# Retention and a mixture of experts on one core: the expert stage issued in program order, with its rows gathered one expert ahead

## The chip, the core and the metric

The kernel runs on one core of a Trainium2 chip. Five engines work there side by side, each through its own queue in order: TensorE (PE, matmuls and transposes into PSUM), VectorE (DVE), ScalarE (ACT), GpSimd (POOL) and SyncE (SP). SP issues most DMAs, POOL the indirect ones (gathers and scatters of rows by index). The metric is the device time of one execution in microseconds; the median of several executions counts. In the profile, L216 is line 216 of the kernel, and PEld is PE's loading of weights, which runs beside its matmuls.

## The reference

Two steps. Retention: for every batch and head a state decays by gamma and collects k times v, and the output is q times the state. Its result, as 3072 rows of 512, goes to eight experts. Each row goes to the one expert whose embedding lies nearest; that expert's two layers are applied to it and the result is scaled by the softmax weight of that expert.

```python
for t in range(S):                       # B, H, S, D = 4, 8, 768, 64
    state = gamma[None, :, None, None] * state + np.einsum('bhd,bhe->bhde', k[:, :, t], v[:, :, t])
    y[:, :, t] = scale * np.einsum('bhd,bhde->bhe', q[:, :, t], state)
...
N, D = x.shape                           # 3072, 512; E, F = 8, 1024
logits = xn @ en.T / tau
expert_idx = np.argmax(logits, axis=1)
...
gate_w = probs[np.arange(N), expert_idx]
for e in range(E):
    mask = expert_idx == e
    h = np.maximum(x[mask] @ w1[e], 0.0)
    out[mask] = gate_w[mask, None] * (h @ w2[e])
```

## The kernel before

**Retention** takes the first 150 us: 24 chunks of 128 tokens, four batches of six chunks. Every chunk's result is written to a table of rows in DRAM (`xd`), its logits are computed, and counts and ranks place each token in the list of its expert. The first expert starts early, on 288 of its 416 rows (`EARLY`); its other 128 (`LATE`) are known only when the last chunk is placed. The generator `products` yields the first layer's products for the early rows one at a time, and `run(m)` takes m of them to fill PE while the last chunk is chosen, ranked and counted (`counting`, which also sorts the experts by their number of tokens and makes the index lists `tidx` for gathering and `sidx` for scattering). The late rows then go through the first layer as rows (`hr`, two halves of 512 columns), are transposed, and join the early ones in `hh` and `hl`.

**The experts** follow in order of their number of tokens, with fixed capacities of 416, 416, 408, 400, 392 and three times 384 rows (`CAPS`). All products are made in three parts for precision: each weight piece of 128 x 1024 is split into a high part (`whi`, a copy on ACT, L191) and a rest (`wlo`, a subtraction on DVE, L192), and so are the rows (`xh`, `xl`) and the hidden values (`hh`, ACT's ReLU at L219; `hl`, DVE at L220). An expert has eight pieces, four for each layer. `load_piece` asks for the next piece on SP (`raw`, six buffers in two pools), `split_piece` splits it (nine pairs of buffers).

- First layer (`first_layer`, L216): eight blocks of 128 hidden units, 12 products each, through four PSUM banks (`psc0`, `psc1`, `py`, `pst`) that `bank` gives in turn.
- Second layer, the first five experts (`layer2`, L1024): four quarters of 128 output columns, 24 products each. DVE transposes each quarter into `yt` (L1026). `finish` copies `yt` into rows (`og`, 16 DMAs on SP, L1034), POOL multiplies by the gates (L1040) and scatters to the output (L1046). Where a capacity is no multiple of 32, the bank's last columns are zeroed first (L1018).
- Second layer, the last three (`layer2_rows`, L1059): three groups of 128 rows; DVE applies the gate (L1061) and POOL scatters.
- The next expert's rows: `gather` (POOL, L959) brings rows from `xd` into `xr`; `to_quarters` writes them to DRAM (`xs`, L969 and L971) and reads them back as `xg` (L980) in a form that DVE's transpose of 32 x 32 blocks turns into columns (`xt`, L1005); `xh` and `xl` follow (L1010, L1011). `xr` has one buffer.

Gates: `gates` sums the squares of the rows, takes their norm, scales the logits (`zd`), and turns them into `gate`, one weight per token. It is written transposed (`gT`) to `gd` and as a column into `xd`. The first two experts gather their gates from `gd` (`gather_gates`, L991), the others find theirs in the gathered rows.

**What sets the order.** Up to the late rows, all engines issue in the order of the program text (`manual_schedule` over all five engines). In the expert stage only SP and POOL do; PE, DVE and ACT are ordered by a scheduler that simulates the program and lets instructions pass each other:

```python
        cx.enter_context(tc.manual_schedule(engines={mybir.EngineType.SP, mybir.EngineType.Pool}))
```

Work written under the two schedules can still be merged by the scheduler. In the text, expert e's turn begins with the gather for expert e + 1, then come the blocks of its first layer with a step of the former expert's `finish` after each and a split and a load after every second, and `to_quarters` for e + 1 after the fifth and the seventh block; then the quarters of its second layer, with a split and a load each.

## Time and profile before

| what | us |
|---|---|
| median of 3 executions | 470.42 |
| lowest, highest | 466.7, 471.93 |
| the profiled execution | 465.52 |
| its span, from the first to the last instruction | 463.7 |
| PE busy in it | 425.4 |
| expert stage: first product of expert 1 to the last product | 191.2 to 450.8 |

A row of the timeline has its start, its duration, engine, line and operation, what it writes from what, and in brackets how long the engine was idle ahead of it and what ended that. An `x8` behind a row means eight instructions merged. A row of the chain of waits has start, duration and what it was. A matmul's duration overlaps the next one's; the distance of starts tells its cost. The clock is TensorE's as granted (1.00 is full speed).

### The profile page before, as it was taken

The numbers are of one execution on the slowest core, as the hardware profiler recorded it, in microseconds if no ns is written. First come the engines' busy times: TensorE is split into PE (matmuls) and PEld (weight loads), VectorE is DVE, ScalarE is ACT, GpSimd is POOL, SyncE is SP. The second block draws the span as 40 slices with busy tenths as digits, with TensorE's granted clock in tenths as the row PEclk, the third lists the DMA queues.
The fourth block names the chain that finished last, engine by engine and source line by source line (L and its number), as shares of the span: only waits on it lengthen the run. The fifth ranks groups of instructions, "written<-read, shape, count | busy, mean of one in ns | idle before, by whom it ended". The sixth has DMA issues, their size and how long they took to land.

```text
span 463.7 us, 8893 instructions
## 1 busy us (share of the span) xinstructions
PE 425.4 (92%) x3230; PEld 381.2 (82%) x3230; DVE 266.7 (58%) x583; ACT 197.9 (43%) x467; POOL 201.4 (43%) x196
## 2 busy tenths in 40 slices
PE   8999999999989889899998999999799999979980
PEld 4787788787868869799997999999799889849860
DVE  5644687868779765764573484293383575346110
ACT  3567668665655152624243253262252353133100
POOL 2545667565545032067282362552553643402010
PEclk9999999999999899999999899999899999999995
DMA  8999999999742236959947948957877892591010
GB/s 200 232 235 241 253 218 260 252 232 248 173 114 47 71 116 208 317 127 289 297 121 214 303 156 203 293 222 187 256 270 188 247 343 77 164 253 66 1 48 20
DMA packets 124441, 89.99 MB, mean 194 GB/s; under 512 B 61680, under 2 KB 106120, under 8 KB 124388
## 3 DMA queue, kind: packets, MB, share of 16 engines
q1 hardware_dynamic: 119972, 75.59, 61.5%
q0 software_dynamic: 4416, 13.75, 9.5%
q8 instruction: 27, 0.44, 0.4%
q14 instruction: 26, 0.21, 0.1%
HBM read 65.89 MB, written 19.39 MB: 184 GB/s over the span
## 4 chain that ended last, share of the span: by engine, by line
PE 32%; DMA 29%; DVE 16%; issue 6%; SPq 6%; ACT 4%; POOL 3%; POOLq 0%; DVEq 0%; ACTq 0%
DMA raw<-in_moe_w_dram 7%; PE psc L216 6%; DMA xg<-xs 5%; DMA xs<-xr 3%; DMA out_dram<-og,sidx 3%; DMA xr<-xd,tidx 3%; PE py L216 3%; PE py L355 3%; DVE wlo L192 2%; SPq L1034 2%; PE pst L216 2%; DMA hh<-in_q_dram 2%; PE psc L1024 2%; PE py L346 2%; PE py L1024 2%
## 5 line engine op out<-in xcount | busy, mean ns | idle before, releaser
L192 DVE TENSOR_TENSOR wlo<-raw,whi 128x1024 fp32r<-128x1024 f32 x59 | 71.8, 1245 | 52.8 <-ACT whi L191 52.4
L191 ACT CAST whi<-raw 128x1024 fp32r<-128x1024 f32 (+1 forms) x69 | 65.0, 984 | 55.5 <-DMA raw<-in_moe_w_dram 55.2
L1046 POOL DMA_INDIRECT out_dram<-og,sidx x29 | 36.1, 1245 | 97.1 <-DMA out_dram<-og,sidx 39.0
L1040 POOL TENSOR_SCALAR og<-og,gt 128x512 f32<-128x512 f32 (+4 forms) x20 | 37.8, 1889 | 37.3 <-DMA og<-yt 36.1
L216 PE MATMUL psc<-xh,whi 128*128 128x384 f32 (+5 forms) x128 | 44.1, 345 | 1.5 <-ACT xh L1010 1.5
L216 PE MATMUL psc<-xl,whi 128*128 128x384 f32 (+5 forms) x128 | 44.3, 346 | 0.7 <-DVE xl L1011 0.7
L216 PE MATMUL psc<-xh,wlo 128*128 128x384 f32 (+5 forms) x128 | 43.8, 342 | 0.0
L280 POOL TENSOR_TENSOR ks<-kin,cst 128x512 f32<-128x512 f32 x23 | 25.1, 1090 | 33.7 <-DMA kin<-in_k_dram 16.4
L959 POOL DMA_INDIRECT xr<-xd,tidx x25 | 29.5, 1179 | 23.3 <-DVE ssq L1073 16.1
L318 DVE TENSOR_TENSOR pm<-psc,cst 128x512 f32<-128x512 f32 x48 | 30.8, 682 | 10.4 <-PE psc L311 10.2
L1024 PE MATMUL psc<-hh,whi 128*128 128x416 f32 (+3 forms) x80 | 29.3, 373 | 6.7 <-ACT hh L219 5.8
L383 ACT ACTIVATE sq<-x 128x128 bf16<-128x128 f32 x96 | 29.8, 310 | 12.4 <-DVE x L369 10.1
L1010 ACT CAST xh<-xt 128x384 fp32r<-128x384 f32 (+4 forms) x28 | 13.8, 522 | 47.7 <-DVE xt L1005 47.7
L220 DVE SCALAR_TENSOR_TENSOR hl<-psc,hh 128x384 fp32r<-128x384 f32 (+5 forms) x32 | 17.0, 549 | 25.5 <-ACT hh L219 25.5
L219 ACT ACTIVATE hh<-psc 128x384 fp32r<-128x384 f32 (+5 forms) x32 | 15.4, 487 | 36.2 <-PE psc L216 36.2
L1024 PE MATMUL psc<-hl,whi 128*128 128x416 f32 (+3 forms) x80 | 28.7, 361 | 0.1
L1005 DVE STREAM_TRANSPOSE xt<-xg 128x416 f32<-128x416 f32 (+1 forms) x28 | 15.3, 573 | 23.4 <-DMA xg<-xs 23.4
L1024 PE MATMUL psc<-hh,wlo 128*128 128x416 f32 (+3 forms) x80 | 28.7, 361 | 0.0
L311 PE MATMUL psc<-qT,kT 64*128 64x128 f32 x384 | 28.0, 285 | 0.5 <-ACT kT L300 0.5
L355 PE MATMUL py<-pm,vin 128*64 128x128 f32 x368 | 27.3, 280 | 1.0 <-DVE pm L318 0.9
L311 PEld LDWEIGHTS psc<-qT,kT 64*128 64x128 f32 x384 | 23.4, 187 | 4.3 <-issue 3.1
L216 PEld LDWEIGHTS psc<-xh,whi 128*128 128x128 f32 x128 | 24.8, 194 | 2.4 <-ACT xh L1010 2.2
(296 smaller groups left out, 1075.9 us busy)
## 6 DMA issues: line engine op xcount, KB each, us to landing
raw<-in_moe_w_dram SPq DMA_DIRECT2D x60, 512.0 KB, 6.5
vin<-in_v_dram SPq DMA_DIRECT2D x24, 256.0 KB, 4.8
xd<-x SPq DMA_DIRECT2D x48, 128.0 KB, 3.9
kin<-in_k_dram SPq DMA_DIRECT2D x23, 256.0 KB, 4.6
hh<-in_q_dram SPq DMA_DIRECT2D x11, 512.0 KB, 5.8
xs<-xr SPq DMA_DIRECT2D x7, 768.0 KB
xg<-xs SPq DMA_DIRECT2D x16, 208.0 KB, 3.9
og<-yt SPq DMA_DIRECT2D x60, 48.0 KB, 5.1
```

The costliest lines, as they stand in the source:

```text
L191: nc.scalar.copy(out=hv, in_=rv)
L192: eng.tensor_tensor(out=lv, in0=rv, in1=hv.bitcast(F32), op=ALU.subtract)
L216: nc.tensor.matmul(acc[:, :w], a[:, f], x[:, kt, cols], start=(n == 0), stop=(n == 3 * KT - 1))
L280: eng.tensor_tensor(out=scaled[n][:, h], in0=loaded[n][0][:, h], in1=sc[:, h], op=ALU.mult)
L311: nc.tensor.matmul(psc[par][:, j, :], kT[r, j, :], qT[r, j, :], start=True, stop=True)
L318: nc.vector.tensor_tensor(out=pm, in0=psc[par], in1=C("causal").unsqueeze(1).broadcast_to([P, KT, P]), op=ALU.mult)
L355: nc.tensor.matmul(py[a * D:(a + 1) * D, j, :], vi[:, h, :], pt[a][:, j, :], start=(c == 0 and j == 0), stop=True, skip_group_check=True)
L383: nc.scalar.activation(out=sq, in_=xo[:, g], func=AF.Square, accum_out=ssq4[:, n, g:g + 1])
L959: nc.gpsimd.indirect_dma_start(out=xr[:n, j, :], out_offset=None, in_=xd[:, :], in_offset=bass.IndirectOffsetOnAxis(ap=tidx[:n, j, e:e + 1 ...
L1024: nc.tensor.matmul(acc[:, :c], a[:, f], x[:, kt, :c], start=(n == 0), stop=(n == 3 * FT - 1))
L1040: nc.gpsimd.tensor_scalar(out=og[:n, j], in0=og[:n, j], scalar1=gts[e][:n, j:j + 1], scalar2=None, op0=ALU.mult)
L1046: nc.gpsimd.indirect_dma_start(out=out[:, :], out_offset=bass.IndirectOffsetOnAxis(ap=sidx[:n, j, e:e + 1], axis=0), in_=og[:n, j, :], in_ ...
```

## The change

1. The expert stage is issued in program order on all five engines, and the text is written in the order wanted: within a block of the first layer the split and the load of a weight piece stand after the block's products and ahead of its ReLU; in a quarter of the second layer come products, split, the next expert's columns (in pairs, both transposes ahead of both subtractions), the quarter's own transpose, and the load. Four loads stand ahead of the first expert's second layer, not six.
2. Rows are gathered one expert ahead: while expert e works, `gather(e + 2)` is issued behind the first step of `to_quarters(e + 1)`, which moves to the first block (the second step to the third block). The steps of `finish` fall on the other blocks.
3. The zeroing of the banks' last columns (`bank2`) moves to the end of the first layer for three of the four quarters.
4. `gates` moves up, to the late rows of the first expert, and is cut into steps: squares and norm ahead of the late rows, the exponential after their first half, the sum and its transpose after the second. `gather_gates` for experts 0 and 1 moves up to the first expert; `gt` has three buffers.
5. 12 of the early products run ahead of the counts. The late rows' first layer is kept in `sbd`, the retention state's two buffers, and no longer in the retention pool's `qs`.
6. The first expert's first quarter of layer 2 is cut into columns 0 to 288 and 288 to 416.
7. One set of four banks serves everything (`bank()`), and the raw pieces change pools one piece later.

The core of the diff:

```diff
+        run(R[3])
         todo2 = counting()
-        for _ in range(19):
+        for i in range(19):
             next(todo2)
-            run(2)
+            run(2 if i < 15 else 0)
...
-        run(R[3])
+        run(DF)
+        gate_steps = gates()
+        next(gate_steps)
...
-            hr.append(ap_.tile([P, H, D], F32, name="qs").rearrange("p h d -> p (h d)"))
+            hr.append(sbd[len(hr)].rearrange("p j d -> p (j d)"))
             nc.scalar.copy(out=hr[-1][:LATE], in_=acc[:LATE])
             split_piece()
-        run(DF)
+            next(gate_steps)
...
-        raw_pool = lambda g: (rp, rp2)[(g - NPE) // 3 % 2]
+        raw_pool = lambda g: (rp2, rp)[(g - NPE - 1) // 3 % 2]
...
-        cx.enter_context(tc.manual_schedule(engines={mybir.EngineType.SP, mybir.EngineType.Pool}))
+        cx.enter_context(tc.manual_schedule(engines={
+            mybir.EngineType.PE, mybir.EngineType.DVE, mybir.EngineType.Activation, mybir.EngineType.Pool,
+            mybir.EngineType.SP}))
         steps = iter(())
+        gather(1)
+        to_go = to_quarters(1)
         for e in range(NE):
...
             if e == 0:
                 hh, hl = hh0, hl0
-                for _ in range(3):
+                for _ in range(4):
                     load_piece()
-                gate_steps = gates()
+                next(to_go)
                 next(gate_steps)
-                for _ in range(3):
-                    next(todo, None)
-                    load_piece()
+                gather_gates(0)
+                gather(2)
+                gather_gates(1)
             else:
...
+                to_go = to_quarters(e + 1) if nxt else iter(())
                 for ft in range(FT):
-                    for _ in first_layer(e, ft, bank("acc"), *xTs[e], hh, hl, slice(0, CAPS[e])):
-                        pass
-                    next(steps, None)
+                    products = first_layer(e, ft, bank(), *xTs[e], hh, hl, slice(0, CAPS[e]))
+                    for _ in range(3 * KT):
+                        next(products)
+                    if ft == FT - 1 and CAPS[e] % P:
+                        accs += [bank2(e) for _ in range(KT - 1)]
                     if ft % 2 == 1:
-                        weights()
-                    if ft in (4, 6):
-                        next(todo, None)
+                        split_piece()
+                        load_piece()
+                    next(products, None)
+                    if ft == 0:
+                        next(to_go, None)
+                        if e + 2 < NE:
+                            gather(e + 2)
+                    if ft == 2:
+                        next(to_go, None)
+                    else:
+                        next(steps, None)
...
                 for dt in range(KT):
-                    layer2(e, dt, hh, hl, yt)
-                    if nxt:
-                        for kt in ((), (0, 1), (2, 3), ())[dt]:
-                            xT_piece(e + 1, kt)
-                    with tc.issue_after(evac.ins) if e == 0 else nullcontext():
-                        weights()
+                    cols = [slice(0, EARLY), slice(EARLY, CAPS[e])] if (e, dt) == (0, 0) else [slice(0, CAPS[e])]
+                    acc = accs[dt]
+                    layer2(e, dt, hh, hl, acc, cols)
+                    split_piece()
+                    if nxt and dt in (1, 2):
+                        xT_pieces(e + 1, (2 * dt - 2, 2 * dt - 1))
+                    to_yt(e, dt, acc, yt)
+                    if (e, dt) == (0, 0):
+                        next(to_go)
+                    load_piece()
                 steps = finish(e, yt, og)
             else:
                 for j, n in groups_of(e):
-                    layer2_rows(e, j, n, hh, hl, og)
-                    if nxt:
-                        for kt in ((0,), (1, 2), (3,))[j]:
-                            xT_piece(e + 1, kt)
+                    acc = layer2_rows(e, j, n, hh, hl)
                     for _ in range((2, 1, 1)[j]):
-                        weights()
+                        split_piece()
+                    if nxt and j > 0:
+                        xT_pieces(e + 1, (2 * j - 2, 2 * j - 1))
+                    rows_out(e, j, n, acc, og)
+                    for _ in range((2, 1, 1)[j]):
+                        load_piece()
```

Three places in the instructions. First ACT, from the last blocks of expert 2's first layer (408 columns) into its second layer; `raw` pieces of 128x1024 belong to a first layer, those of 128x8x4x32 to a second. Before:

```order
L219 ACTIVATE hh_3382<-psc1_3508 128x408
L219 ACTIVATE hh_3382<-py_3529 128x408
L191 CAST whi_3642<-raw_3367 128x1024
L191 CAST whi_3683<-raw_3426 128x1024
L191 CAST whi_3726<-raw_3486 128x1024
L219 ACTIVATE hh_3382<-pst_3549 128x408
L191 CAST whi_3785<-raw_3527 128x8x4x32
L1010 CAST xh_3571<-xt_3634 128x400
```

The same place on ACT now:

```order
L219 ACTIVATE hh_3390<-psc0_3565 128x408
L191 CAST whi_3599<-raw_3388 128x8x4x32
L219 ACTIVATE hh_3390<-psc1_3580 128x408
L191 CAST whi_3637<-raw_3456 128x1024
L191 CAST whi_3668<-raw_3501 128x1024
L1041 CAST xh_3608<-xt_3672 128x400
L1041 CAST xh_3608<-xt_3675 128x400
L191 CAST whi_3707<-raw_3561 128x1024
```

Before, three splits for expert 3's first layer stand ahead of the last block's ReLU; now one split for expert 2's own second layer does, and those for expert 3 stand behind the ReLU.

Second POOL, the gather of expert 7's rows (three indirect DMAs into `xr`) and what stands ahead of it; `og_4291` and `og_4325` are expert 4's output rows, `og_4649` and `og_4677` expert 5's. Before:

```order
L1040 TENSOR_SCALAR og_4291<-og_4291,gt_3868 8x512
L1046 DMA out_0_dram<-og_4291,sidx_82 3072x512
L974 COPY gt_4585<-xr_4453 128x3
L1046 DMA out_0_dram<-og_4649,sidx_82 3072x512 x3
L959 DMA xr_4789<-xd_69,tidx_81 128x576 x3
```

The same gather on POOL now:

```order
L1003 COPY gt_4489<-xr_4133 128x3
L988 DMA xr_4491<-xd_69,tidx_81 128x576 x3
L1082 TENSOR_SCALAR og_4325<-og_4325,gt_3772 128x512
L1088 DMA out_0_dram<-og_4325,sidx_82 3072x512
...
L1088 DMA out_0_dram<-og_4677,sidx_82 3072x512 x3
L1003 COPY gt_4825<-xr_4491 128x3
```

The gather of expert 7 moved from behind the scatters of experts 4 and 5 to ahead of both.

Third DVE, after the late rows' first layer; `wlo<-raw` rows are weight splits, `zd`, `gate` and `gT` belong to the gates, `hl<-plg` is the first half of the late rows' hidden values. Before:

```order
L703 TENSOR_TENSOR ov_2718<-cnt_87,cst2_61 1x168
L1073 COPY ssq_74<-pq_2786 32x24 x2
L192 TENSOR_TENSOR wlo_2723<-raw_2013,whi_2722 128x8x4x32
L1073 COPY ssq_74<-pq_2786 32x24 x2
L220 SCALAR_TENSOR_TENSOR hl_112<-pst_2664,hh_2300 128x288
L938 SCALAR_TENSOR_TENSOR hl_112<-plg_2729,hh_2300 128x4x128
```

The same place on DVE now:

```order
L729 TENSOR_TENSOR ov_2738<-cnt_87,cst2_61 1x168
L192 TENSOR_TENSOR wlo_2742<-raw_2013,whi_2741 128x8x4x32
L645 TENSOR_REDUCE gate_83<-zd_73 128x24
L192 TENSOR_TENSOR wlo_2911<-raw_2803,whi_2910 128x1024
L646 TENSOR_SCALAR gate_83<-gate_83 128x24
L647 RECIPROCAL gate_83<-gate_83 128x24
L651 COPY gT_2750<-psc1_2748 24x128
L967 SCALAR_TENSOR_TENSOR hl_112<-plg_2752,hh_2300 128x4x128
```

The gates, and among them the split of the next weight piece, now stand ahead of the late rows' hidden values; before, the gates followed them. On PE the transpose of `gate` likewise stands ahead of the late rows' transposes.

More of the change, by code (lines that the diff above doesn't have):

```diff
@@ L1065, in retention_moe @@
         xTs[0] = (xh0, xl0)
-        def gates():
-            pq = bank("po")
-            nc.tensor.matmul(pq[:, :NB * NQ], quarters, ssq4.rearrange("p n g -> p (n g)"), start=True, stop=True)
-            for g in range(NQ):
-                p = slice(g * Q, (g + 1) * Q)
-                nc.vector.tensor_copy(out=ssq[p], in_=pq[p, g:NB * NQ:NQ])
-            rn = cp.tile([P, NB], F32, name="rn")
-            norm_of(rn, ssq, P, NB)
-            nc.vector.tensor_tensor(out=zd, in0=zd, in1=rn.unsqueeze(2).broadcast_to([P, NB, NE]), op=ALU.mult)
-            nc.scalar.activation(out=zd, in_=zd, func=AF.Exp)
-            nc.vector.tensor_reduce(out=gate, in_=zd, axis=AX.X, op=ALU.add)
-            nc.vector.tensor_scalar(out=gate, in0=gate, scalar1=1e-9, scalar2=None, op0=ALU.add)
-            nc.vector.reciprocal(out=gate, in_=gate)
-            pg = bank("po")
-            nc.tensor.transpose(pg[:NB, :P], gate, ident)
-            gT = cp.tile([NB, P], F32, name="gT")
-            nc.vector.tensor_copy(out=gT, in_=pg[:NB, :P])
-            yield
-            nc.sync.dma_start(out=gd.rearrange("(n p) o -> n (p o)", p=P), in_=gT)
-            nc.sync.dma_start(out=xd[:, DM:DM + 1].rearrange("(n p) o -> p (n o)", p=P), in_=gate)
-            yield
```

103 lines of the change are left out of this document (64 added, 39 removed).

## The prediction, made before the result was known

> **What bounds the kernel now.** I read the page's engine shares first, then PE's waits over the expert stage, then the stretches around each wait, and last the rows ahead of each wait on the engine that released it.
>
> ```profile
> PE 425.4 (92%) x3230; PEld 381.2 (82%) x3230; DVE 266.7 (58%) x583; ACT 197.9 (43%) x467; POOL 201.4 (43%) x196
> PEclk9999999999999899999999899999899999999995
> ...
> PE psc L1024 <- ACT hh L219: 5.8, 2, 2.9
> PE py L216 <- ACT xh L1010: 2.9, 2, 2.6
> PE px L644 <- DVE cum L529: 2.2, 1, 2.2
> PE psc L216 <- ACT xh L1010: 1.5, 2, 1.3
> ...
> PE psc L216 <- DVE xl L1011: 0.7, 3, 0.3
> PE py L216 <- DVE xl L1011: 0.4, 1, 0.4
> ```
>
> PE is busy 92% of the span; no other engine passes 58%. PE has work for nearly the whole span, so a microsecond in which it waits is a microsecond of the span. The lower rows are PE's waits from 140 us to the end (engine, line, releaser: sum, times, longest). Those on L216 and L1024 that end on L219, L1010 and L1011 belong to the experts 1 to 7 and sum to 5.8 + 2.9 + 1.5 + 0.7 + 0.4 = 11.3 us. The clock row falls to 8 in three slices of 11.6 us; a fourth dip (416.1, below) lies across two slices. The stretches show why:
>
> ```profile
> 153.30:156.70 3.40, 3.40 (x16) 3.40 (x15) 1.72 (x8) 0.80 (x2) 0.11 (x1) 0.50 0.30 87
> ...
> 252.30:255.70 3.40, 0.66 (x4) 0.31 (x2) 0.33 (x1) 1.41 (x2) 3.07 (x3) 1.00 1.04 371
> 255.70:259.10 3.40, 3.30 (x10) 3.22 (x11) 1.45 (x3) 0.68 (x2) 0.48 (x1) 0.50 0.95 311
> 259.10:327.60 68.50, 68.50 (x377) 67.84 (x375) 38.50 (x61) 25.07 (x38) 30.51 (x25) 1.00 0.76 218
> 330.80:334.20 3.40, 3.40 (x12) 3.40 (x12) 1.68 (x4) 1.04 (x1) 0.48 (x2) 0.50 0.91 291
> ...
> 412.70:416.10 3.40, 1.68 (x7) 1.10 (x7) 3.23 (x7) 1.57 (x4) 0.00 (x0) 1.00 0.92 338
> 416.10:419.50 3.40, 3.00 (x9) 2.60 (x10) 3.40 (x6) 3.40 (x5) 1.10 (x1) 0.50 0.23 86
> ```
>
> Columns: stretch, length, busy time of PE, PEld, DVE, ACT, POOL, then PE's clock, DMA share, GB/s. Two stretches of 3.4 us in which PE was busy for 0.66 and 1.68 us are shown, each followed by 3.4 us at clock 0.50; the dips at 153.3 and 330.8 follow the 2.2 us wait of L644 and the second of L1024's in the same way. Half speed for 3.4 us costs 1.7 us of work, so a wait of 2.2 to 2.9 us costs about 4 to 4.6 us in all. Between two dips PE runs 68.5 us without a hole: the work itself can be fed.
>
> **The change, part by part.** *Program order on ACT, DVE, PE.* The first long wait, in expert 2:
>
> ```profile
> 242.38 7.59 SPq L1034 DMA_DIRECT2D og<-yt  x8
> 250.24 0.37 SPq L167 DMA_DIRECT2D raw<-in_moe_w_dram  x1
> 254.29 1.04 ACT L191 CAST whi<-raw 128x1024 fp32r<-128x1024 f32 x1 [3.79 <-DMA raw<-in_moe_w_dram]
> 255.24 0.50 ACT L219 ACTIVATE hh<-pst 128x408 fp32r<-128x408 f32 x1
> 255.80 0.71 PE L1024 MATMUL psc<-hh,whi 128*128 128x408 f32 x1 [2.84 <-ACT hh L219]
> ...
> 311.13 5.13 SPq L1034 DMA_DIRECT2D og<-yt  x8
> ...
> raw<-in_moe_w_dram SPq DMA_DIRECT2D x60, 512.0 KB, 6.5
> ```
>
> SP spends 7.59 us on eight og copies and only then asks for the weight piece (250.24). ACT sits at that piece's split until 254.29, and the ReLU which PE needs stands behind it. Expert 4 repeats it (2.94 us). The three splits there belong to the next expert's first layer. An expert is eight times 24 products (eight blocks of 12, then four quarters of 24) of about 0.185 us (0.19 for 416 columns, below), 35 us, so nothing needs these splits for some 18 us. In the new order they stand behind the ReLU, one in each quarter of the second layer, and only a split of a piece asked for long before stands ahead of it. Both waits go: 5.8 us, and two dips, 3.4.
>
> What can be late next is that split's load. Fewer loads stand ahead of the og copies now (four pieces ahead, not six), and the four xg DMAs go in among them. The last first-layer piece is asked for after 16 og, 4 xg, 2 xs and 3 loads: 25 issues, at most 7.59/8 = 0.95 us each, and 0.64 where the queue runs freely (5.13 us for 8): 16 to 24 us into the expert, landing 6.5 us later. It is split in the last quarter of the second layer, at 31 us. At 0.64 us for an issue the margin is 8 us, at 0.95 half a microsecond. I take the lower half, a margin of 4 us or more: the slow eight shared the queue with one load just ahead of them, and now loads and og copies alternate in smaller lots.
>
> *Rows gathered one expert ahead.* The wait at expert 7:
>
> ```profile
> 393.34 0.98 POOL L1046 DMA_INDIRECT out_dram<-og,sidx  x1 [2.51 <-DMA out_dram<-og,sidx]
> 394.62 1.56 POOL L959 DMA_INDIRECT xr<-xd,tidx  x1 [0.30 <-issue]
> ...
> 412.69 1.04 DVE L1005 STREAM_TRANSPOSE xt<-xg 128x384 f32<-128x384 f32 x2 [2.35 <-DMA xg<-xs]
> 413.92 0.45 PE L216 MATMUL py<-xh,whi 128*128 128x384 f32 x1 [2.56 <-ACT xh L1010]
> ```
>
> The gather stood on POOL behind expert 5's scatters and started at 394.62; its rows reached DVE 18 us later. Now it stands ahead of expert 4's scatters, some 35 us earlier in POOL's work, and the copy through DRAM starts with the first block of expert 6. Of 18 us of chain nothing is left uncovered: 2.9 + 0.4 us and a dip, 1.7. Behind a gather that waits on POOL stand only gate products and scatters, which feed the output; two og buffers give them an expert's length (35 us). The fourth block's early memsets (under 0.1 us each) are off PE's path; I cost them at nothing, and at most 12 x 0.1 = 1.2 us if DVE were late, which at 58% it is not.
>
> *The first expert.* Its part of the sum is the least sure, so here is the chain.
>
> ```profile
> 156.45 0.46 DVE L220 SCALAR_TENSOR_TENSOR hl<-psc,hh 128x288 fp32r<-128x288 f32 x1 [1.12 <-ACT hh L219]
> 160.00 1.46 PE pst L216 x11
> 161.55 0.42 DVE L913 TENSOR_TENSOR xl<-px,xh 128x256 fp32r<-128x256 f32 x1
> 164.52 2.80 PE pq L924 x12
> 165.09 1.05 ACT L191 CAST whi<-raw 128x1024 fp32r<-128x1024 f32 x1
> 166.18 1.23 DVE L192 TENSOR_TENSOR wlo<-raw,whi 128x1024 fp32r<-128x1024 f32 x1 [3.23 <-ACT whi L191]
> 167.39 0.59 ACT L928 COPY qs<-pq 128x512 f32<-128x512 f32 x1 [1.25 <-PE pq L924]
> 169.53 1.88 POOL L959 DMA_INDIRECT xr<-xd,tidx  x1 [16.11 <-DVE ssq L1073]
> 171.95 0.68 DVE L938 SCALAR_TENSOR_TENSOR hl<-px,hh 128x512 fp32r<-128x512 f32 x1
> 175.02 1.28 ACT L1077 ACT_TABLE_LOAD   x1
> 178.18 0.36 ACT L1077 ACTIVATE zd<-zd 128x192 f32<-128x192 f32 x1 [1.88 <-DVE zd L1076]
> 179.57 0.30 DVE L1080 RECIPROCAL gate<-gate 128x24 f32<-128x24 f32 x1
> 189.38 0.35 PE L1024 MATMUL pst<-hl,whi 128*128 128x416 f32 x1
> 189.57 0.35 PE L1024 MATMUL pst<-hh,wlo 128*128 128x416 f32 x1
> ```
>
> The 12 products (1.46/11 = 0.133 us apart, 1.6 us) that now go ahead of the counts cover most of the 2.2 us wait at 152.56, and its dip (1.7) goes. The counts on DVE then lose the 1.12 us wait at 156.45, but start 0.45 later behind an hl: the late rows' xl is done near 161.0 instead of 161.97, and the late rows' 24 products (2.80/12 = 0.233 us each) end near 166.4, against 167.32. While PE waits for xl, twelve products of layer 2 run.
>
> Then the gates stand in front. On ACT table load (1.28) and exp come ahead of the second copy, and exp needs zd, which on DVE stands behind the wlo of piece 6 (165.4 + 1.2); exp ends near 167.4, the copy at 167.9, the split of piece 7 at 168.9 on ACT and 170.2 on DVE. There stand gate's three steps (0.3 each at most) and among them the wlo of piece 8 (1.2): 172.2. Only now can PE transpose gate, and the late rows' transposes, ReLU and hl follow. Those took from 167.98 (the copy's end) to 172.63 (the last hl's end), 4.65 us with a wlo of 1.2 among them: 3.4 without, to 175.6. The late columns' 24 products run beside the hl and end near 176.2 (an estimate: about 0.06 us each, as 128 columns less take 0.057 off 0.19). Three quarters of layer 2 remain: 72 x 0.19 (189.38 to 189.57) = 13.7, to 189.9. Before, the last of them started at 189.57 and ended at 189.9. So this stage gives nothing: what the earlier start wins, PE's wait for the gates (some 4 us from 167 to 172) loses. Ends: 3 us better if DVE gets through sooner, 3 worse with a dip there (1.7) and piece 9 late, whose split stands ahead of the ReLU on ACT.
>
> What does gain is expert 1's rows. Their gather waited until 169.53 for a buffer over the late rows' `qs`; the late rows now use `sbd`, so it starts when tidx is ready, near 161.5. Its chain took 169.53 to 189.95 and ends by 182; the 1.5 + 0.7 us of waits at the start of experts 1 and 2 go.
>
> **The sum.** 11.3 us of waits and three dips of 1.7: 16.4; first expert 0. The profiled execution took 465.52 us (span 463.7): 449.1 remain, and as no order written by hand is without a new small wait, 449.5. That execution is 4.9 us below the median of the runs shown (470.42). Waits whose cost hangs on the moment explain part of such a spread and now go, so I carry half of it over: **452 us**.
>
> The Trainium skill, TensorE: Matmul & The Clock Gate (Why this matters for your kernels), advises "No PE-idle gaps >~3µs between matmul bursts"; its Part 1 gives an idle window of about 3.4 us as the way to half speed. This trace halves the clock after waits of 2.2 to 2.9 us, so the measurement decides; by the page the dips would not belong to the waits.
>
> **The rivals.**
> - *The first expert loses more.* If piece 9 lands 5 us later than the chain above needs, or PE's 4 us wait brings two dips, expert 1 starts 3 to 8 us later: 455 to 460 us. For it: three splits and one load stand ahead of the ReLU. Against: piece 9 is asked for near 159 and needed near 170.
> - *The dips stay.* If the half clock comes at moments of its own and not from the waits, its 5.1 us stay: 452 + 5.1 = 457. Against: each dip follows a stretch at least half empty. It is what the page's limit would give, since no wait here reaches it.
> - *The weights become late, no change.* If the queue takes 0.95 us for each issue throughout and loads land a few us later than 6.5, the last first-layer piece is late in three or four experts, and ACT, in strict order, holds the next ReLU behind it: 4 x 4.6 = 18 us come back, 466 to 471.
> - *Slower.* The same, but in all seven experts: 7 x 4.6 = 32 against 16.4 won, some 486 us. It decides where a load lands more than 8 us later than reckoned, over twice its 6.5 us. DMA shares near 1.0 in some stretches speak for it, 0.76 over the long one against.
>
> **How the numbers follow.** Forecast as worked out (446 to 456): 0.62. The first expert loses more: 0.17. The dips stay: 0.06. No change: 0.08. Slower: 0.04. Better than 446: 0.03. The range 445 to 463 leaves out the last three and little else. A measurement of this kernel can tell about 1% from no change. Faster by over 1% (below 465.7): 0.62 + 0.17 + 0.06 + 0.03 = 0.88; within 1%: 0.08; slower: 0.04.
>
> **What would show it.** Right: PE without a wait over 0.5 us from expert 1's start to the last product, no clock of 0.5 after 180 us, ReLUs on ACT waiting only for PE, expert 7's gather some 35 us earlier. The stage before: PE idle some 4 us ahead of gate's transpose, expert 1 starting within 2 us of 190. Wrong: ACT waiting for raw in the experts, or expert 1's first product after 194.

## The result and the profile after

| | median us | lowest, highest | executions |
|---|---|---|---|
| before | 469.94 | 466.7, 471.93 | 4 |
| after | 451.82 | 449.63, 452.95 | 4 |

The ratio is 0.9615, with a 95% interval of 0.9549 to 0.9681: 3.9% faster. Executions more than 1.5% above the fastest of their kernel are left out of the ratios in this document; the farthest took 587.17 us at a granted clock of 0.65, in the run with the planner free. The forecast was 452. The profiled execution of the changed kernel took 449.63 us (its span 447.7), where the prediction's sum for one profiled execution gave 449.5. How its terms stand is another matter, and most of what follows is about that.

The page of the changed kernel, its engine shares and its clock row (each digit is a slice of 11.2 us):

```profile
PE 419.5 (94%) x3254; PEld 379.2 (85%) x3254; DVE 268.2 (60%) x583; ACT 198.3 (44%) x467; POOL 195.1 (44%) x196
...
PEclk9999999999999999999999999999999999999996
```

PE's busy time fell by 5.9 us and no slice of the clock row shows a dip (the one step of half clock that is left, at 176.98, lies across two slices); the 6 at the end lies behind the last product. Two rows of the stretches, one from each trace, show experts 1 to 7 from the end of expert 0's last product to the end of the last product of all (columns as in the prediction). Before:

```profile
189.90:450.80 260.90, 249.47 (x1273) 234.90 (x1272) 135.89 (x203) 90.91 (x136) 107.87 (x86) 0.98 0.68 202
```

After:

```profile
192.49:434.55 242.06, 241.94 (x1273) 231.37 (x1272) 137.52 (x197) 90.28 (x134) 92.42 (x75) 1.00 0.69 208
```

The same 1273 matmul records in 242.06 us instead of 260.90, and PE is idle for 0.12 us of them instead of 11.43. Nothing is left to win in this stretch but the products themselves. What PE still waits for lies at the end of the retention stage and in the first expert; PE's waits of the changed kernel from 140 us on:

```profile
PE py L1061 <- ACT whi L191: 1.3, 1, 1.3
PE psc L649 <- DVE gate L647: 1.0, 1, 1.0
PE py L1061 <- DVE wlo L192: 0.7, 1, 0.7
PE px L670 <- DVE cum L529: 0.5, 1, 0.5
...
PE py L1061 <- DVE hl L967: 0.4, 1, 0.4
```

The half clock that follows these waits is in the stretches of that place:

```profile
166.74:170.15 3.41, 1.94 (x11) 1.32 (x9) 2.09 (x7) 3.15 (x5) 0.00 (x0) 1.00 0.40 143
170.15:173.57 3.42, 1.84 (x13) 1.48 (x13) 2.56 (x6) 1.43 (x3) 0.00 (x0) 1.00 0.69 249
173.57:176.98 3.41, 2.76 (x23) 2.51 (x22) 1.77 (x5) 0.79 (x2) 1.96 (x2) 1.00 0.48 9
176.98:180.40 3.42, 3.42 (x13) 3.29 (x12) 1.72 (x2) 0.00 (x0) 2.69 (x3) 0.50 0.42 66
```

Three stretches with holes, then one step of 3.4 us at 0.50: the only one before the last product. The chain behind these waits, from the timeline of all engines:

```profile
167.61 0.36 ACT L643 ACTIVATE zd<-zd 128x192 f32<-128x192 f32 x1 [0.26 <-DVE zd L642]
...
172.16 0.30 DVE L647 RECIPROCAL gate<-gate 128x24 f32<-128x24 f32 x1
...
172.52 0.28 PE L649 MATMUL psc<-ident,gate 128*24 128x128 f32 x1 [1.03 <-DVE gate L647]
...
174.51 0.68 DVE L967 SCALAR_TENSOR_TENSOR hl<-px,hh 128x512 fp32r<-128x512 f32 x1
```

Where the 16.0 us of span went, by stage (the wait of L644, now L670, marks the end of the retention stage; each time is from a row of the two traces):

| stage | before | after | change | forecast |
|---|---|---|---|---|
| to the wait of L644 / L670 | 152.56 | 153.30 | +0.74 | 0 |
| from there to expert 0's last product | 37.34 | 39.19 | +1.85 | 0, with ends of 3 |
| experts 1 to 7 | 260.90 | 242.06 | -18.84 | -16.4 |
| behind the last product | 12.90 | 13.15 | +0.25 | 0 |
| sum | 463.7 | 447.7 | -16.0 | -16.4, with 0.4 kept for a new wait |

### The profile page after: what moved, and what is told of

Its sections match the earlier page's. It is cut to its first block, busy times and chain, and to the rows that moved or that the text cites. A ratio compares the mean times of both kernels' runs of the same rounds, so it can differ in the third digit from the quotient of the medians.

```text
span 447.7 us, 8900 instructions
## 1 busy us (share of the span) xinstructions
PE 419.5 (94%) x3254; PEld 379.2 (85%) x3254; DVE 268.2 (60%) x583; ACT 198.3 (44%) x467; POOL 195.1 (44%) x196
## 4 chain that ended last, share of the span: by engine, by line
PE 64%; DVE 14%; DMA 6%; issue 6%; POOL 3%; SPq 2%; ACT 1%; POOLq 0%; DVEq 0%; ACTq 0%
PE psc L216 14%; PE psc L1061 8%; PE pst L216 7%; PE py L216 6%; PE py L1061 5%; PE psc L1101 5%; PE pst L1061 4%; PE py L1101 4%; DMA xd<-x 3%; PE pst L1101 2%; DVE pm L318 2%; PE py L355 2%; PE psc L311 1%; SPq L375 1%; POOL qs L273 1%
## 5 line engine op out<-in xcount | busy, mean ns | idle before, releaser
L1088 POOL DMA_INDIRECT out_dram<-og,sidx x29 | 31.2, 1075 | 88.1 <-DVE og L1106 34.5
L191 ACT CAST whi<-raw 128x1024 fp32r<-128x1024 f32 (+1 forms) x69 | 66.7, 982 | 5.8 <-DMA raw<-in_moe_w_dram 5.6
L1082 POOL TENSOR_SCALAR og<-og,gt 128x512 f32<-128x512 f32 (+4 forms) x20 | 39.8, 1990 | 54.6 <-DMA og<-yt 47.0
L216 PE MATMUL psc<-xl,whi 128*128 128x384 f32 (+5 forms) x128 | 43.2, 337 | 0.0
L280 POOL TENSOR_TENSOR ks<-kin,cst 128x512 f32<-128x512 f32 x23 | 24.0, 1042 | 33.5 <-DMA kin<-in_k_dram 31.2
L318 DVE TENSOR_TENSOR pm<-psc,cst 128x512 f32<-128x512 f32 x48 | 30.7, 680 | 11.5 <-PE psc L311 11.3
L988 POOL DMA_INDIRECT xr<-xd,tidx x25 | 25.7, 1029 | 18.7 <-DVE xl L940 7.3
L1061 PE MATMUL psc<-hh,whi 128*128 128x416 f32 (+3 forms) x80 | 27.7, 347 | 0.0
L1061 PE MATMUL psc<-hl,whi 128*128 128x416 f32 (+3 forms) x80 | 27.6, 346 | 0.0
L219 ACT ACTIVATE hh<-py 128x384 fp32r<-128x384 f32 (+5 forms) x16 | 7.8, 488 | 43.2 <-PE py L216 38.2
L355 PEld LDWEIGHTS py<-pm,vin 128*64 128x64 f32 x368 | 20.8, 136 | 6.2 <-DVE pm L318 3.5
```

The costliest lines, as they stand in the source:

```text
L191: nc.scalar.copy(out=hv, in_=rv)
L216: nc.tensor.matmul(acc[:, :w], a[:, f], x[:, kt, cols], start=(n == 0), stop=(n == 3 * KT - 1))
L318: nc.vector.tensor_tensor(out=pm, in0=psc[par], in1=C("causal").unsqueeze(1).broadcast_to([P, KT, P]), op=ALU.mult)
L355: nc.tensor.matmul(py[a * D:(a + 1) * D, j, :], vi[:, h, :], pt[a][:, j, :], start=(c == 0 and j == 0), stop=True, skip_group_check=True)
L988: nc.gpsimd.indirect_dma_start(out=xr[:n, j, :], out_offset=None, in_=xd[:, :], in_offset=bass.IndirectOffsetOnAxis(ap=tidx[:n, j, e:e + 1 ...
L1061: nc.tensor.matmul(acc[:, r], a[:, f], x[:, kt, r], start=(n == 0), stop=(n == 3 * FT - 1), skip_group_check=True)
```

## The experiments

The prediction priced three parts one by one and added them: the order on PE, DVE and ACT (5.8 us of waits and two dips), the earlier rows (3.3 us and a dip, and 2.2 us at two starts), the early memsets (nothing). The theory to begin with was that these prices stand. The rivals: only one of the parts pays, or the parts do nothing alone. Medians are compared with those of the kernel before, executed beside them on the same chip. Differences to the changed kernel's 451.82 are mostly between chips and so good to a few microseconds only (its own executions run from 449.63 to 454.81). Parts 5 to 7 of the change were not tried by themselves. "The planner" is the scheduler that simulates the program; a "dip" is one step of half clock, about 3.4 us.

### The order alone

```diff
-        cx.enter_context(tc.manual_schedule(engines={mybir.EngineType.SP, mybir.EngineType.Pool}))
+        cx.enter_context(tc.manual_schedule(engines={
+            mybir.EngineType.PE, mybir.EngineType.DVE, mybir.EngineType.Activation, mybir.EngineType.Pool,
+            mybir.EngineType.SP}))
```

> The kernel before with one edit: program order on all five engines in the expert stage; rows, memsets and gates stand where they stood. Theory (the strict order on ACT is what ends the ReLU waits): the 5.8 us that PE waits for hh and their two half-clock stretches go, some 9 us; the 2.9 + 0.4 us and one half-clock stretch at expert 7 stay, since the gather still stands behind expert 5's scatters: about 460 to 462 us beside 470, ratio 0.98. Rival (what pays is the earlier gather and the new place of the splits, the order alone gives nothing or moves the waits to the rows): within 1% of the kernel before.

Measured: 556.75 us against 467.98, ratio 1.1945 (1.1886 to 1.2004). Neither theory came near: the order that was to bring 9 us costs 89. The largest of PE's waits in this kernel:

```profile
PE py L1024 <- DVE py L1018: 17.2, 3, 5.8
PE pst L1024 <- DVE pst L1018: 17.1, 3, 5.7
PE psc L1024 <- DVE psc L1018: 15.5, 6, 3.2
```

L1018 is the memset that clears a bank's last columns. Its place in DVE's queue, from the timeline of DVE:

```profile
279.99 0.62 DVE L1026 STREAM_TRANSPOSE yt<-psc 128x416 f32<-128x416 f32 x1 [4.79 <-PE psc L1024]
280.53 0.57 DVE L1005 STREAM_TRANSPOSE xt<-xg 128x416 f32<-128x416 f32 x1
...
284.38 1.23 DVE L192 TENSOR_TENSOR wlo<-raw,whi 128x1024 fp32r<-128x1024 f32 x1 [0.37 <-ACT whi L191]
285.61 0.07 DVE L1018 MEMSET py<- 128x8 f32 x1
```

The memset itself takes 0.07 us. But in the text it opens a quarter, behind the transpose of the quarter before (which waits for PE), four steps of the next rows and a split's rest: DVE reaches it 5.6 us after it began to transpose the quarter that PE had ended, and PE waits for it. The planner had let the memset pass all of that. So a line of the text that was free under the planner becomes the longest wait of the kernel once its order is taken at its word.

### The early memsets undone

```diff
-                    if ft == FT - 1 and CAPS[e] % P:
-                        accs += [bank2(e) for _ in range(KT - 1)]
...
-                while len(accs) < KT:
-                    accs.append(bank2(e))
                 for dt in range(KT):
...
-                    acc = accs[dt]
+                    acc = bank2(e)
```

> The changed kernel with only the early memsets undone: each quarter of a second layer clears its own bank's rest, behind what DVE has ahead of it in the text. Forecast of the prediction: at most 1.2 us. Theory after the run with the order alone: in experts 2, 3 and 4 PE waits 3 to 6 us for the memset at each of three or four quarters, 35 to 60 us of waits and half clock on top, 495 to 530 us. Rival (the rows taken in in pairs and in their new place leave DVE time for the memsets): under 460 us.

Measured: 463.83 us (one execution; the changed kernel's median beside it is 451.82). Both forecasts missed. PE's waits on the memset (here L1050):

```profile
PE psc L1061 <- DVE psc L1050: 4.7, 6, 0.8
PE py L1061 <- DVE py L1050: 4.1, 3, 1.4
PE pst L1061 <- DVE pst L1050: 2.4, 3, 0.8
```

Twelve waits of 0.9 us on average, 11.2 us in all, and no half clock behind any of them. They are far shorter than with the order alone, since the new text takes the rows in ahead of the quarter's transpose, in pairs, and leaves only that transpose ahead of the memset. So the early memsets are worth about 12 us to this kernel. The prediction's 1.2 us was the memsets' own duration; their price is what they queue behind.

### The order and the early memsets, in the old text

```diff
-        cx.enter_context(tc.manual_schedule(engines={mybir.EngineType.SP, mybir.EngineType.Pool}))
+        cx.enter_context(tc.manual_schedule(engines={
+            mybir.EngineType.PE, mybir.EngineType.DVE, mybir.EngineType.Activation, mybir.EngineType.Pool,
+            mybir.EngineType.SP}))
...
+                        if ft == FT - 1 and i == 3 * KT - 1 and CAPS[e] % P:
+                            accs += [bank2(e) for _ in range(KT - 1)]
```

> The kernel before with two edits: program order on all five engines in the expert stage, and the banks' rest cleared ahead of the last ReLU of the first layer, as in the changed kernel; rows, splits, gates and loads stand in the old text. Theory (the order needs all of the new text, the memsets are only the largest piece): the 50 us of waits for memsets go, the waits for the gates' reciprocal (7.3 us) and for splits (8.6 us) stay, some 20 us of waits and half clock behind them: 480 to 500 us. Rival (the memsets were all that was wrong with the order): 455 to 463 us.

Measured: 500.7 us against 470.37 (one execution each). The memset waits are gone, and the time is 56 us below that of the order alone, but the kernel is still 6% slower than before: just beyond the theory's range of 480 to 500 by size, and not all by place. The gates' wait stayed at 7.3 us; the rest has a new form, at the start of an expert. DVE first, then ACT, then PE, each from its own timeline:

```profile
234.37 0.61 DVE L1005 STREAM_TRANSPOSE xt<-xg 128x416 f32<-128x416 f32 x1 [7.69 <-DMA xg<-xs]
```

```profile
242.70 1.99 ACT L191 CAST whi<-raw 128x1024 fp32r<-128x1024 f32 x2
```

```profile
243.80 0.71 PE L216 MATMUL psc<-xh,whi 128*128 128x408 f32 x1 [3.77 <-ACT whi L191]
```

DVE sits 7.7 us in front of rows that have not landed. Quarter transposes stand behind it in the old text, ACT's splits behind its copies of these rows, and PE ends up waiting for a weight split that needed nothing but its turn. In strict order a late row is not one wait, it holds everything behind it on two engines.

### The planner free, in the new text

The counterpart: all of the change stays, but PE, DVE and ACT are the planner's again.

```diff
-        cx.enter_context(tc.manual_schedule(engines={
-            mybir.EngineType.PE, mybir.EngineType.DVE, mybir.EngineType.Activation, mybir.EngineType.Pool,
-            mybir.EngineType.SP}))
+        cx.enter_context(tc.manual_schedule(engines={mybir.EngineType.SP, mybir.EngineType.Pool}))
```

> The changed kernel with the planner free again on PE, DVE and ACT in the expert stage (only SP and POOL in program order); text, early gather and early gates stay. Theory (the order carries 9 to 11 us of the gain): waits of 2 us and more for a ReLU come back in some experts, 458 to 464 us, ratio 0.975 to 0.985. Rival (the text with the gather one expert ahead does it, whoever orders): 450 to 454 us, ratio 0.96, PE without a wait over 0.5 us in experts 1 to 7.

Measured: 467.71 us against 467.98, ratio 1.0017 (0.9984 to 1.005). Neither: the new text without the order gives nothing at all, less than the theory left it. The longest wait, on ACT and on PE:

```profile
213.16 1.04 ACT L191 CAST whi<-raw 128x1024 fp32r<-128x1024 f32 x1 [11.12 <-DMA raw<-in_moe_w_dram]
...
216.01 0.71 PE L216 MATMUL psc<-xh,whi 128*128 128x416 f32 x1 [4.99 <-DVE hl L220]
```

The planner pulls a split ahead of four ReLUs; the piece, which SP asks for at 205.67 behind four `og` copies, lands 11 us after ACT has begun to wait. The changed text asks for four pieces ahead instead of six, which suits a planner less that splits as early as it can; this reading of why it gives nothing was not tried by itself.

So the two halves of the change are worth +89 us and 0 us alone, and -18 us together. Prices of parts that share queues do not add.

### The splits ahead of the ReLU again

The mechanism behind the first 5.8 us, put back alone: in experts 1 to 7, three of the four splits of the second layer stand ahead of the last ReLU of the first layer.

```diff
+                    if ft == FT - 1:
+                        for _ in range(3):
+                            split_piece()
                     next(products, None)
...
-                    split_piece()
+                    if e == 0 or dt == 3:
+                        split_piece()
...
-                    for _ in range((2, 1, 1)[j]):
+                    for _ in range((0, 0, 1)[j]):
                         split_piece()
```

> The changed kernel with one thing put back: three of the four second-layer splits of the next expert's pieces stand ahead of the last ReLU of the first layer, as the planner had put them. Theory (a split that waits for its load holds the ReLU, and PE with it): ACT waits 2 us or more for raw ahead of that ReLU in at least two experts, PE waits 2 us or more there, 458 to 475 us. Rival (the splits cost nothing there, since the products of the earlier hidden blocks cover them): within 1 us of the changed kernel.

Measured: 478.42 us against 467.98, ratio 1.0229 (1.0181 to 1.0277): 27 us over the changed kernel's 451.82, just beyond the theory's range; the rival falls. One of four such places:

```profile
262.11 1.04 ACT L191 CAST whi<-raw 128x1024 fp32r<-128x1024 f32 x1 [3.72 <-DMA raw<-in_moe_w_dram]
...
263.06 0.50 ACT L219 ACTIVATE hh<-psc 128x408 fp32r<-128x408 f32 x1
...
263.62 0.45 PE L1061 MATMUL py<-hh,whi 128*128 128x408 f32 x1 [3.80 <-ACT hh L219]
```

This is the prediction's chain, a load, a split, a ReLU and PE, in the new kernel with one step moved. It shows that the place of the splits keeps these waits out of the new kernel. That they come at four places here and came at two in the kernel before, and cost 27 us and not some 9, may lie in the loads, of which four instead of six run ahead; this was not tried by itself.

### The rows gathered as late as before

```diff
-                gather(2)
                 gather_gates(1)
...
+                if nxt:
+                    gather(e + 1)
+                    to_go = to_quarters(e + 1)
...
-                    if ft == 0:
-                        next(to_go, None)
-                        if e + 2 < NE:
-                            gather(e + 2)
-                    if ft == 2:
+                    if ft in (4, 6):
                         next(to_go, None)
```

> The changed kernel with the rows gathered as late as before: expert e+1's gather at the start of expert e, its copies through DRAM at groups 4 and 6. Theory as predicted: only expert 7 pays, 3.3 us of wait and one half-clock stretch of 1.7 us: 457 us, ratio 0.972. Rival 1 (in strict order late rows hold DVE and ACT, and with them PE, in every expert): waits of 1 us and more at the start of three or more experts, 462 us or over. Rival 2 (the chain was hidden anyway): within 1 us of the changed kernel, ratio 0.96.

Measured: 457.55 us against 467.98, ratio 0.9791 (0.9765 to 0.9817), 5.7 us over the changed kernel's median of 451.82. The theory's 457 holds (against another chip's median), and its place too. DVE's waits for the rows of experts 4 and 7, and PE's longer one at expert 7, from their timelines:

```profile
293.17 1.10 DVE L1039 STREAM_TRANSPOSE xt<-xg 128x416 f32<-128x416 f32 x2 [3.84 <-DMA xg<-xs]
...
401.29 1.04 DVE L1039 STREAM_TRANSPOSE xt<-xg 128x384 f32<-128x384 f32 x2 [3.30 <-DMA xg<-xs]
```

```profile
406.40 0.45 PE L216 MATMUL psc<-xh,whi 128*128 128x384 f32 x1 [2.15 <-ACT xh L1041]
```

PE waits 2.7 us at expert 7 and nowhere else in experts 1 to 7, and one step of half clock follows. That is 4.4 us in the trace; the rest of the 5.7 was not placed, and the half clock behind the first expert lasted three steps in this trace and one in that of the changed kernel. DVE waits once for each expert's rows, 19.3 us in all, and six of these seven waits reach no product. The likely reason, read from the order of the text: a quarter's split now stands ahead of its rows, so little that PE needs soon queues behind them, where 7.7 us of the same wait held PE for 3.8 in the old text.

### Waits of a chosen length

```diff
-                    products = first_layer(e, ft, bank(), *xTs[e], hh, hl, slice(0, CAPS[e]))
+                    acc = held if ft == 5 else bank()
+                    products = first_layer(e, ft, acc, *xTs[e], hh, hl, slice(0, CAPS[e]))
...
+                    if ft == 4:
+                        held = bank()
+                        m = (0, 0, 1, 2, 3, 4, 6, 0)[e]
+                        for i in range(m):
+                            nc.vector.tensor_copy(out=held[:, :384], in_=held[:, :384] if i else acc[:, :384])
```

> The changed kernel with a wait for PE ahead of group 5 of the first layer in experts 2 to 6: 1, 2, 3, 4 and 6 copies on DVE in a row, each some 0.5 us, from the bank that PE has just filled into the next one; results as before. PE should wait about 0.8, 1.3, 1.8, 2.3 and 3.3 us, 9.5 us in all. Theory (a wait of about 2 us or more in a stretch otherwise full brings 3.4 us of half clock): half clock after the last two and perhaps the third, none after the first two. Rival 1 (it takes an idle time near or over 3 us): only after the last. Rival 2 (half clock comes at moments of its own): dips elsewhere too, none tied to the waits.

In each of experts 2 to 6 the copies on DVE hold the bank that PE's sixth block of the first layer needs. Measured: 471.37 us (one execution). PE's five waits were 0.66, 1.26, 1.86, 2.46 and 3.66 us. The stretches around the last three:

```profile
317.44:320.86 3.42, 1.56 (x9) 1.24 (x8) 2.32 (x6) 1.22 (x2) 0.00 (x0) 1.00 1.16 236
...
354.99:358.40 3.41, 0.95 (x6) 0.81 (x5) 3.13 (x6) 1.42 (x2) 0.00 (x0) 1.00 1.13 247
358.40:361.82 3.42, 3.42 (x12) 3.42 (x12) 0.83 (x2) 0.49 (x1) 0.00 (x0) 0.50 1.05 303
392.54:395.95 3.41, 0.43 (x3) 0.10 (x1) 2.81 (x5) 1.42 (x2) 0.21 (x1) 1.00 0.60 221
...
399.36:402.78 3.42, 3.42 (x12) 3.42 (x12) 0.56 (x1) 0.49 (x1) 1.18 (x2) 0.50 0.68 222
```

The row at 317.44 holds the wait of 1.86 us, those at 354.99 and 392.54 the two longer ones, and the rows behind these are at 0.50. No half clock after 0.66, 1.26 and 1.86 us; one step after 2.46; two after 3.66; none elsewhere in experts 1 to 7. The theory holds and both rivals fall: the dips belong to the waits, and a wait of 2.46 us, with PE busy 0.95 us of that stretch, is enough.

### The gates behind the late rows

A kernel that should beat both: the gates' exp, reduction, reciprocal and transpose behind the late rows, and pieces 8 and 9 split behind the late ReLU (ordered by `issue_after`, which the change had dropped).

```diff
             split_piece()
-            next(gate_steps)
...
+        next(gate_steps)
+        next(gate_steps)
         for _ in todo2:
...
                     layer2(e, dt, hh, hl, acc, cols)
-                    split_piece()
+                    with tc.issue_after(evac.ins) if e == 0 else nullcontext():
+                        split_piece()
```

> The changed kernel with the gates' exp, reduction, reciprocal and transpose behind the late rows' transposes, ReLU and hl, and the splits of pieces 8 and 9 behind that ReLU too. Theory (the first expert pays some 4 us of waits and a half-clock stretch of 1.7 us because the gates and two splits stand in front of the late rows): these waits fall under 1.5 us, no clock of 0.5 between 160 and 190 us, expert 1's first product 3 to 5 us earlier, 447 to 449 us, ratio 0.950 to 0.957. Rival (the waits move on to the pieces' splits or to late gates): expert 1 starts within 1 us of the changed kernel, ratio 0.96.

Measured: 456.71 us against 469.31, ratio 0.9757 (0.97 to 0.9815), slower than the changed kernel's 451.82. The long waits in the first expert did go (0.7 and 0.4 us are left of them); a longer one came. The timelines of SP, DVE and PE:

```profile
180.04 0.34 SPq L653 DMA_DIRECT2D gd<-gT  x1
...
180.94 2.95 SPq L1010 DMA_DIRECT2D xg<-xs  x4
```

```profile
193.15 1.11 DVE L1040 STREAM_TRANSPOSE xt<-xg 128x416 f32<-128x416 f32 x2 [12.64 <-DMA xg<-xs]
```

```profile
189.18 0.35 PE L1062 MATMUL psc<-hh,wlo 128*128 128x416 f32 x1
194.44 0.71 PE L216 MATMUL py<-xh,whi 128*128 128x416 f32 x1 [4.91 <-ACT xh L1042]
```

On SP the gates' copy stands ahead of the four copies that bring expert 1's rows, so later gates make later rows. In the changed kernel these copies were issued at 174.04, 20.7 us after the wait of L670 that ends the retention stage (153.30); here at 180.94, 25.5 us after it (155.43). PE waits 4.9 and then 1.1 us, with three steps of half clock. Counted from the same point, expert 1 starts after 39.0 us, and after 39.2 in the changed kernel: the rival's sign, a start within 1 us, is what came.

### The rows ahead of the gates on SP

The same, with these four copies ahead of the gates' two, and expert 1's rows taken in behind the splits of pieces 8 to 11:

```diff
                 next(to_go)
+                next(to_go)
                 next(gate_steps)
...
-                    if nxt and dt in (1, 2):
-                        xT_pieces(e + 1, (2 * dt - 2, 2 * dt - 1))
+                    for i in ((), (0,), (1,), ())[dt] if e else ((), (), (), (0, 1))[dt]:
+                        xT_pieces(e + 1, (2 * i, 2 * i + 1))
...
-                    if (e, dt) == (0, 0):
-                        next(to_go)
```

> As the run with the gates behind, and besides: expert 1's copies out of DRAM are issued ahead of the two gate copies on SP, and its rows are taken in in the last quarter of expert 0's second layer, behind the splits of pieces 8 to 11. Theory (the gates in front of the late rows cost PE 4 us and the half clock behind it, and the only thing that kept the gain from showing was the gate's copy ahead of the rows' copies on SP): xg issued near 176 instead of 181, PE's wait at expert 1's start under 2.5 us, no half clock between 160 and 190 us, 444 to 448 us, ratio 0.945 to 0.955. Rival (the rows land no earlier, since they share the DMA engines with four loads): a wait of 4 us or more at expert 1's start again, 452 us or over.

> The changed kernel once more, unedited, on the chip of the two runs beside it. Theory (its spread comes from how long the half clock lasts after the first expert's waits: one, three or four steps of 3.41 us in the executions seen, 1.7 to 6.8 us): median 451 to 455, executions between 449 and 456, ratio 0.955 to 0.970. Rival (this kernel's time is settled to 0.3%, the chips differ): a ratio outside 0.955 to 0.968.

Measured on one chip: this kernel 447.95 us (six executions, 445.85 to 450.58), the changed kernel 451.82 (six, 449.82 to 454.81), the kernel before 465.94 (eleven). Ratios to before: 0.9634 (0.958 to 0.9687) and 0.9722 (0.9666 to 0.9778). It beats both; the intervals overlap a little, but five of its six executions lie below the changed kernel's fastest. From its timelines of SP and PE, and its page:

```profile
174.66 1.88 SPq L1010 DMA_DIRECT2D xg<-xs  x4
182.04 0.34 SPq L653 DMA_DIRECT2D gd<-gT  x1
```

```profile
188.67 0.35 PE L216 MATMUL py<-xh,whi 128*128 128x416 f32 x1
```

```profile
PEclk9999999999999999999999999999999999999995
```

The rows' copies leave at 174.66 and expert 1 starts at 188.67, 33.9 us after the wait of L670 at 154.76 (39.2 in the changed kernel, as above). PE's waits there sum to 1.9 us, and this execution has no half clock at all before the last product. The time and the mechanism came as the theory had them; the ratio did not (0.9634, not 0.945 to 0.955), since before itself was faster on this chip. The copies ahead of the gates and the later place of expert 1's rows were not tried apart.

The changed kernel's second median is the first one to the digit, 451.82, while the ratio is 0.9722 instead of 0.9615: it is the kernel before whose median moved, from 469.94 to 465.94. So the theory's 451 to 455 holds and its range of ratios just misses. The rival's sign, a ratio outside 0.955 to 0.968, came as well: the chips differ, though the executions spread over 1.1% and not the rival's 0.3%. The gain is 3 to 4%.

## Why the prediction was right, and where it was not

- *PE bounds, and its waits are the gain.* Right. Experts 1 to 7 lost 18.8 us against 16.4 forecast: 11.31 us of idle time (11.3 forecast) and 7.53 us of busy time, where the three dips account for 4.9 (half of the 9.7 us that PE was busy in these steps; the prediction had 5.1). The other 2.7 us are not settled. That a restart after a wait is slow for a product or two (0.45 us at 413.92 in the prediction's rows, at full clock, and 0.34 from the third product on) is in the rows, but was not tried by itself.
- *Program order, 5.8 us and two dips.* The cause was named rightly: with the splits ahead of the ReLU again, the load, the split, the ReLU and PE wait in the same chain as in the kernel before. What failed is that the order was priced as a part that works alone. Alone it costs 89 us; the order needs a text in which what PE waits for does not stand behind work that it does not need.
- *The loads.* Wrong in size, and it did no harm. The margin was put at 4 us or more, from at most 0.95 us for an issue. The trace of after:

```profile
240.85 10.27 SPq L1076 DMA_DIRECT2D og<-yt  x8
...
250.60 1.05 ACT L191 CAST whi<-raw 128x1024 fp32r<-128x1024 f32 x1 [2.10 <-DMA raw<-in_moe_w_dram]
```

  Eight copies took 10.27 us, 1.28 each, and in experts 1 to 5 ACT waited for a load five times, 2.1 us at most. ACT waiting for `raw` in the experts was one of the prediction's own signs of being wrong; it came, and PE did not wait for it. So the rival of late weights was right about the loads and wrong about the price: no ReLU that PE needed at once stood behind such a split. The run with the splits ahead of the ReLU shows what the same loads cost where one does.
- *The early memsets, nothing, at most 1.2 us.* Against the kernel before, that is what the sum needed, since the planner had placed them well. As the price of the step it is wrong by a factor of ten: about 12 us in the new text, 56 in the old. The step that failed is the fallback, which counted durations (12 times 0.1) for an instruction that stands at the end of a queue.
- *Expert 7's rows, 3.3 us and a dip.* Right: 5.7 us by the medians, and 2.7 us and a dip in the trace of the late gather. In the trace of after the gather starts at 343.20 instead of 394.62, 51 us earlier where 35 were reckoned:

```profile
343.20 1.07 POOL L988 DMA_INDIRECT xr<-xd,tidx  x1 [0.27 <-POOL gt L1003]
```

- *The first expert, 0 with ends of 3.* +1.85 us, of which 1.7 is the dip that was named as the worse end. The chain's times came within a microsecond up to the late hl: the exp ended at 167.97 (forecast 167.4), the copy at 168.45 (167.9), gate at 172.46 (172.2), the late hl at 175.19 (175.6). PE's wait was put at 4 us and its waits between 168 and 175 sum to 3.7, but only 1.0 of it stands ahead of gate's transpose, as forecast; 2.0 stand ahead of the split of piece 7 (the waits on `whi` and `wlo`), and 0.7 ahead of the late rows' hidden values. Expert 1 started at 192.50, outside the 2 us around 190 that the prediction gave as a sign of being right. Its rows, reckoned to be in by 182, were taken in by DVE at 186.94; no product waited for them. What the prediction did not see is that the gates' copy on SP ties expert 1's rows to them: an edit that only cures the wait moves it.
- *The dips.* Three of 1.7 us are gone, and the run with chosen waits ties such dips to the waits; the rival that they stay falls. The page of the Trainium skill, TensorE: Matmul & The Clock Gate (Part 1), gives one idle window of about 3.4 us as the way to half speed, and its section Why this matters for your kernels warns of gaps over some 3 us. The measurement decides: 2.46 us were enough here, and the last section has the bound.
- *Half the distance to the median.* It held by its size; its reason holds in part. The first expert's waits are left, and the half clock behind them lasted one step in the profiled execution of after and three in the profiled one of its second measurement: 447.7 and 450.1 us of span.
- *The sum.* 449.5 forecast for the profiled execution and 449.63 measured is in part luck: experts 1 to 7 gave 2.4 us more than reckoned, and the three other stages took back 2.8, where 0.4 was kept for them. The median's agreement to 0.2 us is luck too, since the same kernel's executions spread over 5 us.

## What to carry to other kernels

Going from a planner to program order is one change with its text: before the switch, look in each queue for what stands behind something that can be late without needing it, because from then on it waits too. Price a moved instruction by what it queues behind and who waits for it, not by its duration: twelve memsets of 0.07 us on DVE were worth about 12 us here, and 56 in the old text. When a wait is cured by moving its producer later, follow the producer's other readers through every queue, the DMA queue above all, before counting the gain.

## What the runs showed of the hardware

- The granted clock changes on a grid of 3.41 us (cut on it, the steps of the twelve traces, from 11 us to near the last product, have 1.00 or 0.50 and nothing between), and what nearly always decides is how much of one step PE was busy. Of the steps at full clock, 36 had PE busy for 1.54 us or less, and all 36 were followed by half clock; of 1429 with 1.74 us or more, 4 were; in between both were seen. Two of those 4 are the one dip of the changed kernel (behind a step with 2.76 us) and the same place with the late memsets; the bound does not explain them. So it takes half a step, not an idle one, and a wait costs a dip or not by how it falls across the grid. The same wait of 2.18 us, that of L644, left one emptier step in the kernel before (first row), with half clock behind it, and two fuller ones in the run with the order and the early memsets, with none:

```profile
149.89:153.30 3.41, 1.19 (x11) 0.88 (x9) 2.76 (x15) 0.02 (x1) 1.01 (x1) 1.00 0.00 0
...
148.59:152.00 3.41, 2.85 (x24) 2.47 (x22) 3.23 (x18) 1.52 (x7) 0.00 (x0) 1.00 0.27 69
152.00:155.42 3.42, 1.74 (x14) 1.75 (x15) 2.38 (x12) 0.41 (x1) 1.12 (x1) 1.00 0.11 15
```

  With the planner free, a wait of 3.21 us left 1.97 and 1.64 us in its two steps and brought no dip. The Trainium skill, TensorE: Matmul & The Clock Gate (What's actually happening), says that the window is 3413 ns and runs freely; the grid agrees with it, the bound does not agree with an idle window.
- Coming back took one to four steps, also where PE was busy throughout. From the run with the late gather, the second and third such steps behind the first expert's waits:

```profile
174.86:178.27 3.41, 3.41 (x18) 3.41 (x17) 0.91 (x4) 0.00 (x0) 2.50 (x4) 0.50 0.45 43
178.27:181.68 3.41, 3.41 (x14) 3.31 (x14) 1.72 (x2) 0.00 (x0) 2.80 (x3) 0.50 0.71 138
```

  In six traces whose first expert waits nearly alike (after and its second measurement, the late memsets, the late gather, the splits ahead of the ReLU, the chosen waits) the half clock there lasted 1, 3, 1, 3, 3 and 4 steps: 1.7 to 6.8 us, if half of each step is lost, for nearly the same code.
- Eight copies of `og` took SP between 5.09 and 10.27 us to issue in experts 1 to 5 of after's profiled execution.
